# A fused attention and MoE kernel: the first round of scores starts with six query groups in place of eight, twelve tiles are drained in two halves of the keys, and narrow PSUM units last until unit 30

## The chip, the cores and the metric

The kernel runs on one core of a Trainium2 chip. A time is the device time of one execution of the whole program, in microseconds. The median over the runs shown is what counts; the profile is one further execution, recorded by the hardware profiler. The engines are TensorE (PE, with its weight loads as PEld), VectorE (DVE), ScalarE (ACT), GpSimd (POOL) and SyncE (SP). POOL and SP issue DMAs.

## The reference

An attention over pooled keys is followed by a two-layer network with a quick GELU, on every token.

```python
kv_pool = kv.reshape(B, H // r, r, W // r, r, C).mean(axis=(2, 4))   # r = 4
k = v = kv_pool.reshape(B, -1, C) @ w_sr
a = np.exp(s - s.max(-1, keepdims=True))       # s = (q @ k.T) / sqrt(C)
x = (a / (a.sum(-1, keepdims=True) + 1e-09)) @ v
h = x.reshape(B * S, D) @ w_in
out = (h * (1.0 / (1.0 + np.exp(-1.702 * h)))) @ w_out
```

B is 4, there are 12288 queries to an item, 768 pooled keys, C = 128 channels, and 2048 hidden units in the network. Inputs and output are float32; the kernel computes in bfloat16 with float32 sums.

## The kernel before

**Work and chunks.** The 49152 queries are cut into 96 groups of 512. For attention, a group and one block of 128 keys make a *chunk*: a matmul (`fill_attn`, L333) writes 128 x 512 scores to one PSUM bank. There are six key blocks, so six chunks to a group. For the network (called MoE in the code), a group and 128 of the 2048 hidden units make a chunk (`fill_moe`, L559), sixteen to a group. PSUM has eight banks of 512 float32 to a partition.

**Units.** ACT works on one to three chunks at once, a *unit*: an exponential for scores (L335), a GELU for MoE (L561). Units alternate between the banks 0 to 2 and 3 to 5, so that PE fills one while ACT empties the other. The banks 6 and 7 are accumulators for all other work of PE. A unit's result goes as bfloat16 to a frame of three slots in `ag`, an SBUF buffer of 102 slots. From there PE *drains* it: `drain_attn` (L344) multiplies the exponentials by the values, `drain_moe` (L569) by the second weight matrix. What lies in `ag` undrained is the lead that ACT has over PE.

**Draining.** An attention tile is 128 queries. Three tiles share an accumulator bank of 3 x 129 columns (the last column gives the sum for the softmax). A call `drain_attn(t, a)` does three of the six key blocks for tile t; both halves add up in the same bank. Then DVE takes the reciprocal (L355) and writes the product to `x` (L358). An MoE group of 512 queries sums 16 matmuls in one bank; DVE transposes it to `o_sb` (L580, three buffers) and SP stores it. The last group is drained by small matmuls (`drain_last`, L597), so that its parts can be stored one by one.

**Two rounds.** Groups 0 to 47 go through attention and MoE, then groups 48 to 95. Within the first round, eight groups start side by side: first their key blocks 0 and 1, then block 2 of all eight, block 3, and so on, because the keys arrive one block after another. After that the groups follow one by one. The first 18 units hold 1, 1, eight times 2, 3, 3, and twice 3, 3, 2 chunks, and all after that three (the last nine of the program two).

**Keys and queries at the start.** The first kv item is loaded in six chunks on POOL's DMA queue (`load_chunk`), between loads of the first four tiles of q (`load_q`, in halves or quarters of a tile; a half is two groups). For each kv chunk PE pools (`pool_chunk`, L134), DVE copies, PE makes keys and values (`key_and_value`, L156 and L157), and DVE copies them to SBUF (L158, L159). The queries of groups 0 to 15 are transposed on PE (`transpose_q`, L228) and copied by DVE (L234); later ones are cast to a DRAM buffer by POOL (`cast_q`) and loaded transposed by SP (`load_qT`), at the groups that `CAST` and `TURN` name. `gate` makes POOL wait for a small memset on DVE, so that such loads do not start too early.

**What sets the order.** All instructions are issued in an order that the program computes when it is built. The dictionary `first` names work that is put ahead of a given unit. For the rest a loop over units estimates, with fixed costs (`COST`, `FIXED`, `CHUNK`), when PE and ACT are free. After each `fill` it places drains and extras (pooling, transposing) as long as the next fill would not come late by its estimate (`limit`), or whenever few frames are left. Each engine then executes its own list in order.

**Work that ACT does not do.** Some chunks (`early`, `rolling`, `lent`) are computed on DVE by polynomials (L400 to L442), spread over the span.

## Time and profile before

| | |
|---|---|
| median of 4 runs | 954.76 us (954.69 to 954.86) |
| the profiled execution | 954.86 us |
| its span | 953.1 us |
| ACT busy | 934.6 us |
| PE busy | 941.8 us (ends of matmuls are modelled) |
| DVE busy | 513.1 us |
| first unit on ACT | starts at 9.44 us |
| switches between exponential and GELU | at 143.5, 488.9 and 605.9 us |

The page lists engines, a picture of the span in 40 slices, the chain of work that ended last, and groups of instructions by source line. The timeline gives instructions of one engine in order of time: start, length, engine, line, operation, output and input, how many were merged, and in brackets how long the engine was idle before and what ended that. Times in the trace are counted from the span's start. An ACT instruction is shown from its start to its last write, so the next starts before the one before it has ended; the pitch is the distance from start to start. A wait with several causes is put down to the one that came last.

### The profile page before, as it was taken

How to read it: one execution, taken by the hardware profiler on the slowest of the kernel's cores; microseconds unless marked ns; L12 is line 12 of the kernel's file. 1: busy time of each engine (PE TensorE's matmuls, PEld its weight loads, DVE VectorE, ACT ScalarE, POOL GpSimd, SP SyncE). 2: the span in 40 equal slices, each digit the busy share in tenths (PEclk: the TensorE clock that was granted, in tenths of full speed). 3: DMA queues.
4: the chain of work that ended last, by engine and by line, in shares of the span. 5: the costliest groups of instructions: out<-in, count | busy, mean ns of one | idle time of the engine just before them, and what ended most of it. 6: DMA issues, size and time to landing. Idle time of an engine off the chain costs nothing.

```text
span 953.1 us, 15440 instructions
## 1 busy us (share of the span) xinstructions
PE 941.8 (99%) x6330; PEld 504.1 (53%) x6330; DVE 513.1 (54%) x1004; ACT 934.6 (98%) x703; POOL 68.0 (7%) x118
## 2 busy tenths in 40 slices
PE   7899999999999999999999999999999999999998
PEld 4677777444444444454446777754444444444444
DVE  5443653111677877777545764367656555663011
ACT  5999999999999999999999999999999999999996
POOL 4101101330000332000000000000000000000000
PEclk9999999999999999999999999999999999999999
DMA  9989991999762799215268875563222222222222
GB/s 181 200 163 163 212 215 37 146 142 179 152 122 42 109 148 112 42 24 89 34 98 155 162 162 100 117 125 48 34 44 35 44 34 45 34 45 38 41 41 48
DMA packets 371319, 94.41 MB, mean 99 GB/s; under 512 B 344688, under 2 KB 368880, under 8 KB 370928
## 3 DMA queue, kind: packets, MB, share of 16 engines
q1 hardware_dynamic: 341808, 60.78, 36.8%
q0 software_dynamic: 29168, 32.51, 22.2%
q8 instruction: 49, 0.80, 0.4%
q14 instruction: 22, 0.18, 0.1%
q10 hardware_dynamic: 272, 0.13, 0.0%
HBM read 52.49 MB, written 48.23 MB: 106 GB/s over the span
## 4 chain that ended last, share of the span: by engine, by line
ACT 85%; PE 13%; DMA 1%; issue 0%; DVE 0%; POOL 0%; POOLq 0%
ACT ag L561 71%; ACT ag L335 14%; PE banks L344 6%; PE banks L333 5%; DMA x<-in_kv_dram 1%; PE banks L569 0%; PE banks L559 0%; PE banks L597 0%; PE banks L134 0%; DVE x L358 0%; PE banks L228 0%; ACT L561 0%; ACT L335 0%; POOL x L217 0%; PE banks L280 0%
## 5 line engine op out<-in xcount | busy, mean ns | idle before, releaser
L561 ACT ACTIVATE ag<-banks 128x1536 bf16<-128x1536 f32 (+1 forms) x511 | 683.2, 1507 | 0.0
L559 PE MATMUL banks<-x,w_in_sb 128*128 128x512 bf16 x1524 | 412.3, 379 | 0.1
L569 PE MATMUL banks<-ag,w_out_sb 128*128 128x512 bf16 x1508 | 407.2, 379 | 0.0
L335 ACT ACTIVATE ag<-banks 128x1536 bf16<-128x1536 f32 (+2 forms) x186 | 245.4, 1470 | 3.7 <-PE banks L333 3.6
L569 PEld LDWEIGHTS <-w_out_sb 128*128 128x128 bf16 x1520 | 148.6, 98 | 178.5 <-issue 0.2
L559 PEld LDWEIGHTS <-w_in_sb 128*128 128x128 bf16 x1524 | 147.0, 98 | 168.5 <-issue 2.1
L580 DVE STREAM_TRANSPOSE o_sb<-banks 128x512 f32<-128x512 f32 x95 | 67.9, 715 | 213.1 <-PE banks L569 199.3
L344 PEld LDWEIGHTS <-ag 128*128 128x128 bf16 x2272 | 145.4, 98 | 43.8 <-issue 1.1
L344 PE MATMUL banks<-v,ag 128*128 128x129 bf16 x2272 | 162.7, 220 | 0.2
L333 PE MATMUL banks<-qT,kT 128*128 128x512 bf16 x544 | 147.7, 379 | 4.0 <-ACT ag L335 2.3
L411 DVE SCALAR_TENSOR_TENSOR ea<-ea,eb 128x512 f32<-128x512 f32 x128 | 87.9, 687 | 3.9 <-DVE ea L411 0.8
L355 DVE RECIPROCAL rec<-banks 128x3 f32<-128x3 f32 x128 | 23.0, 180 | 98.4 <-PE banks L344 97.9
L358 DVE TENSOR_TENSOR x<-banks,rec 128x384 bf16<-128x384 f32 x128 | 71.4, 557 | 4.4
L333 PEld LDWEIGHTS <-kT 128*128 128x128 bf16 x544 | 46.7, 98 | 30.5 <-issue 3.9
L168 POOL DMA_DIRECT2D kvs<-in_kv_dram x32 | 40.3, 1299 | 31.0 <-DMA kvs<-in_kv_dram 28.7
L442 DVE RECIPROCAL eb<-ea 128x256 f32<-128x256 f32 x24 | 40.8, 1725 | 0.4
L400 DVE TENSOR_SCALAR ea<-banks 128x512 f32<-128x512 f32 x32 | 22.1, 692 | 33.8 <-PE banks L384 33.8
L490 POOL MEMSET gate_tile<- 1x1 f32 x39 | 4.2, 108 | 427.4 <-DVE gate_tile L489 427.4
L435 DVE SCALAR_TENSOR_TENSOR ea<-ea,eb 128x512 f32<-128x512 f32 x48 | 33.0, 688 | 1.4
L422 DVE TENSOR_SCALAR qT<-banks 128x512 f32<-128x512 f32 x12 | 8.3, 692 | 31.3 <-PE banks L378 31.1
L406 DVE SCALAR_TENSOR_TENSOR eb<-eb,ea 128x512 f32<-128x512 f32 x32 | 22.0, 687 | 0.8
L413 DVE SCALAR_TENSOR_TENSOR ag<-ea,ee 128x512 bf16<-128x512 f32 x24 | 16.6, 690 | 1.1
(80 smaller groups left out, 255.4 us busy)
## 6 DMA issues: line engine op xcount, KB each, us to landing
out_dram<-o_sb SPq DMA_DIRECT2D x380, 64.0 KB, 2.0
kvs<-in_kv_dram POOLq DMA_DIRECT2D x32, 384.0 KB, 6.3
q_bf<-in_q_dram POOLq DMA_DIRECT2D x20, 512.0 KB, 6.6
x_bf<-x SPq DMA_DIRECT2D x11, 768.0 KB, 6.1
x<-in_kv_dram POOLq DMA_DIRECT2D x12, 512.0 KB, 10.9
x_bf<-x SPq DMA_DIRECT2D x10, 384.0 KB, 4.7
x<-in_q_dram POOLq DMA_DIRECT2D x7, 256.0 KB, 15.1
w_in_sb<-in_moe_w_in_dram POOLq DMA_DIRECT2D x1, 512.0 KB, 7.8
```

Source lines behind the costliest of these rows:

```text
L168: nc.gpsimd.dma_start(out=kv_sums[b][:, i2], in_=kv_p[b, i, w, :, i2], **({"accum_op": ADD} if n else {}))
L333: nc.tensor.matmul(ps[:, k, :], kTs[i // GB][:, jc * 128:(jc + 1) * 128], rhs, start=True, stop=True)
L335: nc.scalar.activation(place([("a",) + c for c in chunks]), ps, AF.Exp, scale=scale)
L344: nc.tensor.matmul(av_of[u][:, k * (C + 1):(k + 1) * (C + 1)], weights(("a", i, jc))[:, o:o + T], vs[i // GB][:, jc, 0:C + 1], start=(jc = ...
L358: nc.vector.tensor_tensor(to, ps[:, :, 0:C], rec.unsqueeze(2).broadcast_to([128, TS, C]), MUL)
L411: nc.vector.scalar_tensor_tensor(a, a, COEFFS[k], b, ADD, MUL)
L435: nc.vector.scalar_tensor_tensor(a, a, COEFFS[k], b, ADD, MUL)
L442: nc.vector.reciprocal(b[:, m:m + 256], a[:, m:m + 256])
L559: nc.tensor.matmul(ps[:, k, :], w_in_sb[:, fc * 128:(fc + 1) * 128], x[:, g % (4 * XS) * G:(g % (4 * XS) + 1) * G], start=True, stop=True)
L561: nc.scalar.activation(place([("m",) + c for c in chunks]), ps, AF.Gelu_apprx_sigmoid)
L569: nc.tensor.matmul(o_of[g], w_out_sb[:, fc, :], weights(("m", g, fc)), start=(fc == 0), stop=(fc == FCH - 1))
L580: nc.vector.transpose(o_sb, o_of.pop(g))
```

## The change

- The accumulator may be any of several banks in turn (`turns`): 7, 6 and 5 from the start, and 2 as well from unit 4. Three units before the first unit of three chunks, banks 2 and 5 are taken out again. Bank 2 and 5 are free until then, because all units up to that one hold at most two chunks.
- The sizes of the units are 1, 1, then 28 times 2; from unit 30 on three chunks.
- Six groups start side by side in place of eight.
- The first 12 tiles (`SPLIT` = 4 sets of three) are drained in two halves of the keys: blocks 0 to 2 of all 12 tiles first, copied from PSUM to float32 partial sums (`parts`), then blocks 3 to 5, to which DVE adds the partial sums. The partial sums use the first frames of `ag`, which are kept out of use (`kept`) until the last set is done.
- The second half of q's second tile is loaded after kv chunks 2 to 4 in place of before them. The dictionary `first` names other units, and transpositions of groups 6 to 15 become extras.
- The builder's estimates are changed: how long a bank stays occupied includes DVE's queue (`copied`).
- Four casts and two transposing loads of q move from the last groups of the first attention round to MoE groups 19 to 22, 34 and 38.

```diff
--- before.py
+++ after.py
@@ -78,19 +78,22 @@
     banks = ppool.tile([128, 8, 512], F32, name="banks")
     closes = {}
-    free = {6: 0.0, 7: 0.0}
+    free = {2: 0.0, 5: 0.0, 6: 0.0, 7: 0.0}
+    turns = [7, 6, 5]
     last_acc = 7
     def acc(key=None):
         nonlocal last_acc
         last_acc = next_acc()
+        turns.append(last_acc)
+        turns.remove(last_acc)
         if key:
             closes[last_acc] = key
         return banks[:, last_acc, :]
     def next_acc():
-        return min((m for m in (13 - last_acc, last_acc) if m not in closes), key=lambda m: free[m])
+        return min((m for m in turns if m not in closes), key=lambda m: (max(free[m], now), turns.index(m)))
     def acc_bf():
         return acc().bitcast(BF)
@@ -100,6 +103,8 @@
             del closes[m]
             free[m] = then
+    now = 0.0
     x = xpool.tile([128, XS * SG], BF, name="x")
@@ -241,14 +246,13 @@
     load_chunk(0, 1)
     load_q(0, 2, 4)
     load_q(1, 0, 2)
-    load_q(1, 2, 4)
     for jc in range(2, JC):
         if jc == JC - 1:
-            load_q(2, 0, 2)
+            load_q(1, 2, 4)
         load_chunk(0, jc)
-    load_q(2, 2, 4)
-    load_q(3, 0, 2)
-    load_q(3, 2, 4)
+    for s in range(2, QS):
+        load_q(s, 0, 2)
+        load_q(s, 2, 4)
     cast_q(4)
     ones = cpool.tile([128, 32], BF)
@@ -289,12 +293,15 @@
     slot_of = {}
     low = 0
+    SPLIT = 4
+    kept = (2 * SPLIT + K - 1) // K
+    parts = ag[:, 0:2 * SPLIT, :].rearrange("p (u a) t -> p u (a t)", a=2).bitcast(F32)
     written = [0] * (AG // K)
     order, unit = [], 0
     def free_frames():
         busy = {s // K for s in slot_of.values()}
-        return [f for f in range(low // K, AG // K) if f not in busy]
+        return [f for f in range(max(low // K, kept), AG // K) if f not in busy]
     def place(chunks):
         nonlocal order, unit
@@ -336,21 +343,35 @@
     def drain_attn(t, a):
+        nonlocal kept
         i, u, k = t // 4, t // TS, t % TS
-        if k == a == 0:
+        split = u < SPLIT
+        if k == 0 and (a == 0 or split):
             av_of[u] = acc(("av", u))
         o = t % 4 * T
         for jc in range(a * K, a * K + K):
             nc.tensor.matmul(av_of[u][:, k * (C + 1):(k + 1) * (C + 1)], weights(("a", i, jc))[:, o:o + T],
-                             vs[i // GB][:, jc, 0:C + 1], start=(jc == 0), stop=(jc == JC - 1))
+                             vs[i // GB][:, jc, 0:C + 1], start=(jc == (a * K if split else 0)), stop=(jc == (a * K + K if split else JC) - 1))
             if t % 4 == 3 and (i, jc) in rolling:
                 used.append((i, jc))
             elif t % 4 == 3 and i not in early:
                 del slot_of["a", i, jc]
+        if k == TS - 1 and a == 0 and split:
+            close(("av", u), max(now, dve - 1.0) + 3.2)
+            on_dve(3.0)
+            nc.vector.tensor_copy(parts[:, u, 0:TS * (C + 1)], av_of.pop(u)[:, 0:TS * (C + 1)])
         if k == TS - 1 and a == 1:
             close(("av", u), max(now, dve - 1.0) + EVACUATE)
-            on_dve(4.3)
-            ps = av_of.pop(u)[:, 0:TS * (C + 1)].rearrange("p (k c) -> p k c", k=TS)
+            on_dve(6.5 if split else 4.3)
+            ps = av_of.pop(u)[:, 0:TS * (C + 1)]
+            if split:
+                part = parts[:, u, 0:TS * (C + 1)]
+                nc.vector.tensor_tensor(part, ps, part, ADD)
+                ps = part
+                if u == SPLIT - 1:
+                    kept = 0
+                    order.clear()
+            ps = ps.rearrange("p (k c) -> p k c", k=TS)
             rec = npool.tile([128, TS], F32, name="rec")
             nc.vector.reciprocal(rec, ps[:, :, C])
             n, o = divmod(u * TS, RT)
@@ -489,8 +510,8 @@
         nc.vector.memset(one, 0.0)
         nc.gpsimd.memset(one, 0.0)
-    TURN = {4: 4, 8: 5, 18: 6, 21: 7, 24: 8, 27: 9, 29: 10, 32: 11, 36: 12, 40: 13, 44: 14}
-    CAST = {0: 5, 4: 6, 13: 7, 19: 8, 22: 9, 25: 10, 28: 11, 32: 12, 36: 13, 40: 14, 44: 15, 46: 16}
+    TURN = {4: 4, 8: 5, 18: 6, 21: 7, 24: 8, 27: 9, 29: 10, 32: 11, 36: 12}
+    CAST = {0: 5, 4: 6, 13: 7, 19: 8, 22: 9, 25: 10, 28: 11, 32: 12}
     def background(i):
@@ -535,6 +556,11 @@
             order[:] = [f for f in order if f >= low // K]
         if g == 40:
             background(early[0])
+        if 19 <= g < 23:
+            gate()
+            cast_q(g - 6)
+        if g in (34, 38):
+            load_qT(13 + (g - 34) // 4)
         for b, lo in ((2, 2), (3, 24)):
             if lo <= g < lo + 8:
                 gate()
@@ -610,11 +636,11 @@
     NA, NM = NG * JC, NG * FCH
-    chunks, sizes = [], [1] * 2 + [2] * 8 + [3, 3] + [3, 3, 2] * 2
+    chunks, sizes = [], [1] * 2 + [2] * 28
     chunks += [(0, 0), (1, 0), (0, 1), (1, 1)]
-    chunks += [(i, jc) for i in range(2, 8) for jc in range(2)]
-    chunks += [(i, jc) for jc in range(2, JC) for i in range(8)]
-    chunks += [(i, jc) for i in range(8, NG) for jc in range(JC) if i not in early and (i, jc) not in rolling]
+    chunks += [(i, jc) for i in range(2, 6) for jc in range(2)]
+    chunks += [(i, jc) for jc in range(2, JC) for i in range(6)]
+    chunks += [(i, jc) for i in range(6, NG) for jc in range(JC) if i not in early and (i, jc) not in rolling]
     seq, todo = [], []
     todo_early = [("a", t, a) for t in range(NT) for a in range(2) if (t // TS * TS + TS - 1) // 4 in early]
     for n in range(R):
@@ -623,7 +649,11 @@
             m = sizes.pop(0) if sizes else K
             seq.append(("a", part[:m]))
             part = part[m:]
-        todo += [("a", t, a) for t in range(n * NT // R, (n + 1) * NT // R) for a in range(2)
+        begin = n * NT // R
+        if n == 0:
+            begin = SPLIT * TS
+            todo += [("a", t, a) for a in range(2) for t in range(begin)]
+        todo += [("a", t, a) for t in range(begin, (n + 1) * NT // R) for a in range(2)
                  if (t // TS * TS + TS - 1) // 4 not in early]
         flat = [(g, fc) for g in range(n * NG // R, (n + 1) * NG // R) for fc in range(FCH)]
         todo += [("m",) + c for c in flat]
@@ -634,6 +664,7 @@
             seq.append(("m", flat[:m]))
             flat = flat[m:]
+    narrow = min(p for p, (kind, part) in enumerate(seq) if len(part) == K)
     at = {}
     for p, (kind, part) in enumerate(seq):
         for c in part:
@@ -664,7 +695,7 @@
             f(*args)
             if f in COST:
                 now += COST[f][0]
-                free[last_acc] = now + COST[f][1]
+                free[last_acc] = copied(f)
         kind, part = seq[p]
         for i, jc in part:
             if (kind, i) not in begun:
@@ -674,7 +705,7 @@
                 f, *args = extras.pop(0)
                 now = max(now, free[next_acc()]) + COST[f][0]
                 f(*args)
-                free[last_acc] = now + COST[f][1]
+                free[last_acc] = copied(f)
     first = {
         0: [(pool_chunk, 0, 0), (transpose_q, 0), (warm, 1), (key_chunk, 0, 0), (transpose_q, 1)],
@@ -683,20 +714,17 @@
         3: [(transpose_q, 3)],
         4: [(transpose_q, 4)],
         5: [(transpose_q, 5)],
-        6: [(transpose_q, 6)],
-        7: [(transpose_q, 7)],
-        8: [(pool_chunk, 0, 2)],
-        9: [(key_and_value, 0, 2)],
-        11: [(pool_chunk, 0, 3)],
-        12: [(key_and_value, 0, 3)],
-        13: [(pool_chunk, 0, 4)],
-        14: [(key_and_value, 0, 4)],
-        15: [(transpose_q, 8)],
-        16: [(pool_chunk, 0, 5)],
-        17: [(key_and_value, 0, 5)],
-        18: [(transpose_q, 9)],
-        19: [(transpose_q, 10)],
-        20: [(transpose_q, 11), (later, 12), (later, 13), (later, 14), (later, 15)]}
+        6: [(pool_chunk, 0, 2)],
+        7: [(key_and_value, 0, 2)],
+        9: [(pool_chunk, 0, 3)],
+        10: [(key_and_value, 0, 3)],
+        12: [(pool_chunk, 0, 4)],
+        13: [(key_and_value, 0, 4)],
+        14: [(later, 6)],
+        15: [(pool_chunk, 0, 5)],
+        16: [(key_and_value, 0, 5), (later, 7)],
+        17: [(later, 8)],
+        18: [(later, g) for g in range(9, 16)]}
@@ -705,10 +733,11 @@
     COST = {pool_chunk: (1.9, 2.6), key_chunk: (0.3, 2.4), value_chunk: (0.3, 2.4),
             transpose_q: (1.05, 4.2), early_fill: (1.0, 5.5), key_and_value: (0.55, 3.5),
             transpose_pooled: (0.9, 3.6), make_k: (0.8, 3.2), make_v: (0.8, 3.7)}
+    COPY = {pool_chunk: 1.5, key_chunk: 1.5, value_chunk: 1.5, key_and_value: 2.8, transpose_q: 3.2}
     SMALL = 0.26
     RECIPROCAL = 10.5
     PAUSE = 4.0
-    now, end, extra_at = 0.0, [], 0.0
+    end, extra_at = [], 0.0
     source, dve = None, 0.0
     early_left = 2 * (G // T) * EARLY
@@ -716,6 +745,12 @@
         nonlocal dve
         dve = max(dve, now + 1.0) + cost
+    def copied(f):
+        if f not in COPY:
+            return now + COST[f][1]
+        on_dve(COPY[f])
+        return max(now + COST[f][1], dve)
     def fill(p):
         nonlocal now
@@ -723,6 +758,14 @@
             return
         kind, part = seq[p]
         prepare(p)
+        if p == 4:
+            turns.insert(0, 2)
+        if p == narrow - 3:
+            for m in (2, 5):
+                turns.remove(m)
+        if p == narrow:
+            assert not any(m in closes for m in (2, 5))
+            now = max(now, free.pop(2), free.pop(5))
         lo = K * (p % 2)
         (fill_attn if kind == "a" else fill_moe)(part, banks[:, lo:lo + len(part), :])
         if p >= 2:
@@ -753,7 +796,7 @@
             if f:
                 now = max(now, bank) + COST[f][0]
                 f(*args)
-                free[last_acc] = dve + 1.0 if f is early_fill else now + COST[f][1]
+                free[last_acc] = dve + 1.0 if f is early_fill else copied(f)
                 if f in (transpose_pooled, make_k, make_v):
                     on_dve(2.5)
                 extra_at = max(now + PAUSE, dve + 1.5 if f in (transpose_pooled, make_k, make_v) else 0.0)
@@ -773,8 +816,9 @@
             kind, i, c = source[0]
             needs = at[("at" if kind == "a" else kind, i, c)]
             cost = K * SMALL if kind == "a" else 1.0
-            first_of = c == 0 and (kind == "m" or i % TS == 0)
-            if source is not todo_early and (needs > n or (kind == "a" and first_of and at["at", i + TS - 1, 1] > n)
+            halved = kind == "a" and i // TS < SPLIT
+            first_of = (c == 0 or halved) and (kind == "m" or i % TS == 0)
+            if source is not todo_early and (needs > n or (kind == "a" and first_of and at["at", i + TS - 1, c if halved else 1] > n)
                                              or (kind == "m" and first_of and (i, FCH - 1) in lent
                                                  and made.get((i, FCH - 1), 1e9) > now + 1.0)
                                              or (kind == "a" and (early_waits(i) or first_of and early_waits(i + TS - 1)))):
@@ -795,7 +839,7 @@
                 early_left -= 1
                 if not early_left:
                     low = 0
-            if c == (1 if kind == "a" else FCH - 1) and (kind == "m" or i % TS == TS - 1):
+            if (halved or c == (1 if kind == "a" else FCH - 1)) and (kind == "m" or i % TS == TS - 1):
                 source = None
     assert not todo and not todo_early and not extras and not early_todo

```

## The prediction

> **What bounds the kernel now.** I read the engine totals first, then who ScalarE waits for, then the pitch of ScalarE's instructions, then the two ends of the span.
>
> ```profile
> span 953.1 us, 15440 instructions
> PE 941.8 (99%) x6330; PEld 504.1 (53%) x6330; DVE 513.1 (54%) x1004; ACT 934.6 (98%) x703; POOL 68.0 (7%) x118
> ...
> ACT 85%; PE 13%; DMA 1%; issue 0%; DVE 0%; POOL 0%; POOLq 0%
> ```
>
> ```profile
> ACT ag L335 <- PE banks L333: 3.6, 4, 2.2
> ```
>
> ACT is the bound: in the whole span it waits 3.6 us for scores (L333) in four places. So only three things can move the time: the number and width of ACT's instructions, new or removed waits of ACT, and what follows its last instruction. Pitch, from the ACT timeline and the chain:
>
> ```profile
> 16.08 1.03 ACT L335 ACTIVATE ag<-banks 128x1024 bf16<-128x1024 f32 x1
> ...
> 17.89 1.05 ACT L335 ACTIVATE ag<-banks 128x1024 bf16<-128x1024 f32 x1
> ...
> 284.60 14.63 ACT ag L561 x11
> ```
>
> Two narrow instructions (two chunks of 512) lie between 16.08 and 17.89: 0.904 us each. Eleven wide ones (three chunks) take 14.63: 1.331 each. A chunk thus costs 0.427, an instruction 0.050 besides.
>
> The early part on PE, and the landings of the loads:
>
> ```profile
> 17.59 0.56 PE L134 MATMUL banks<-sum,x 128*128 128x32 bf16 x16
> 18.08 0.59 PE L333 MATMUL banks<-qT,kT 128*128 128x512 bf16 x2
> 18.52 0.22 PE L156 MATMUL banks<-pTc,w_sr_sb 128*128 128x128 bf16 x1
> 18.58 0.22 PE L157 MATMUL banks<-w_sr_sb,pTc 128*128 128x128 bf16 x1
> 19.18 1.53 PE L333 MATMUL banks<-qT,kT 128*128 128x512 bf16 x5 [0.39 <-DVE kT L158]
> ```
>
> ```profile
> 12.36 0.71 POOL L217 DMA_DIRECT2D x<-in_q_dram  x1 [0.71 <-DMA x<-in_q_dram]
> 13.64 0.72 POOL L217 DMA_DIRECT2D x<-in_q_dram  x1 [0.57 <-DMA x<-in_q_dram]
> 14.92 0.70 POOL L217 DMA_DIRECT2D x<-in_q_dram  x1 [0.56 <-DMA x<-in_q_dram]
> 17.40 0.52 POOL L204 DMA_DIRECT2D q_bf<-in_q_dram  x1 [1.79 <-DMA x<-in_kv_dram]
> ```
>
> Each issue waits for the landing of the load eight places before it, and starts 0.28 after that (the trace's landing events: 12.07, 13.35, 14.63, 17.12). So a half tile of q takes 1.28 us in the queue, a chunk of kv 2.49.
>
> The end:
>
> ```profile
> 943.17 0.59 PE L559 MATMUL banks<-x,w_in_sb 128*128 128x512 bf16 x2
> 943.61 1.89 PE L569 MATMUL banks<-ag,w_out_sb 128*128 128x512 bf16 x8
> 945.33 0.67 PE L597 MATMUL banks<-w_out_sb,ag 128*128 128x128 bf16 x9
> 946.30 3.23 PE L597 MATMUL banks<-w_out_sb,ag 128*128 128x128 bf16 x55 [0.30 <-DVE o_sb L580]
> ```
>
> PE issues ACT's last unit at 943.17, and still has 8 output matmuls of 0.213 and all 64 small ones of the last group (0.053 each) to do. ACT ends at 944.96, PE at 949.53: the tail is PE's backlog. That is how work that is off ACT's path still sets the end.
>
> **The change, part by part.** The sum is made against the profiled execution, 954.86 us (span 953.1 and 1.76 around it), which is 0.10 above the median, 954.76.
>
> Narrow units. Round 1 had 2 units of one chunk, 10 of two and 88 of three; it gets 2, 28 and 76. Eighteen narrow ones more and twelve wide ones fewer: 18 x 0.904 - 12 x 1.331 = +0.30 us of ACT, uncovered, since ACT is the bound.
>
> The Trainium skill's page "ScalarE: Activation LUTs", section "What ACT_TABLE_LOAD costs", speaks harder against the change: a fixed 186 to 280 ns an instruction with 93 ns of overlap back to back, so by an estimate from it six more instructions would cost 0.56 to 1.12. The pitch above shows 0.050 each, so I keep 0.30.
>
> Start up to unit 5. The same instructions and the same loads in the same order; only accumulator banks differ. Unit 2 at 13.29 hangs on kv chunk 1 (landed 10.81). No gain: 0.
>
> Keys and values, units 6 to 16. With six groups, chunks 2, 3, 4, 5 of the keys are needed at units 7, 10, 13, 16 instead of 9, 12, 15, 18: dense, at 17.9, 20.6, 23.3 and 26.0 instead of 19.8, 23.4, 27.1 and 30.8. Moving the half tile of q behind them brings each chunk 1.28 earlier: 15.85, 18.28, 21.2, 24.9. From the first pooling matmul to the exponential took 17.59 to 19.82 = 2.23 us, so data are in time to about a third of a microsecond, except the last. But PE is in order. A narrow fill can start when the unit two before it is done (0.05 after its 1.03 us) and needs 0.62 to reach ACT, out of 2 x 0.904: 0.11 us of slack (wide: 0.33). A key/value step costs more: copying kT (L158) holds the fill until 0.66 after the key matmul. Before, this made unit 9 start 0.13 late (18.79, then 19.82). After, drains (attention x values, L344: six matmuls in 0.33) stand ahead of two of these steps, three ahead of another, and pooling (0.42) with a transposition (0.22) and three drains ahead of unit 15. Going along with these durations: unit 7 is 0.25 late, 10: 0.42, 12 and 13: 0.14 and 0.34, 15 and 16: 0.18 and 0.44; sum 1.77. From below: four times 0.13 = 0.52, if the drains hide in the waits. From above: 1.77 + 1.28 = 3.05, if chunk 5 lands as late as now. I take 1.7, as the order of the built program puts the drains in front.
>
> What these replace. Before, ACT loses 0.13, 0.13 and 0.10 at its own three key/value steps (19.8, 27.1, 30.8), and 0.38 at 37.94, where 12 drains and transpositions lie between two fills. The order there is another; I take -0.74, between -0.36 (the last stays in some form) and -0.99 (with 0.25 around 51 and 53).
>
> Two halves of the keys for 12 tiles. Four copies of 128x387 and four additions of the same size on DVE; the nearest row, L358 on 128x384, takes 0.557: 4.5 us in a stretch in which DVE is busy 3.35 of 9.0 us (22 to 31). Hidden by ACT's pace. If that cover is gone, PE's next drain or transposition waits for its bank, as at 36.53 (0.18 us, for L358), and behind it the fills. ACT waits for DVE too, at units 31 and 39, where it reuses frames that the partial sums used; those additions are about 2 us older, so 0.
>
> Later casts and loads. Four casts (0.5 us of POOL each) and two transposing loads leave the last third of round 1 and stand at MoE groups 19 to 22, 34 and 38. On SP two loads get in front of output stores, on POOL four casts behind gates get in front of the adding loads of kv. The load at 430.20 stands in just such a place: it holds SP for 5.51 us, and ACT runs on without a gap (12 units from 424.22 to 440.61). Cost 0; if DVE's output tiles ran out, some 5 us less the 7.1 us of a group times three tiles, still 0.
>
> The tail. The halves let PE drain in its early idle time (busy 6.76 of 9.0 between 22 and 31). In the order of the programs, filled chunks not yet drained are 12 fewer from unit 40 on (46 for 62 at unit 50), and the lead stays: after the last fill none of the 8 output matmuls is left, and 61 small ones for 64. That is 8 x 0.213 + 3 x 0.053 = 1.87 off the path; of the wait of 0.30 for the bank of the last whole group (L580) I estimate 0.15 gone. Taken: -2.0, between -1.7 and -2.2. Stores are no cover for it: the last one is issued right after PE's end and DVE's copy.
>
> Ten of ACT's 61 waits on its own semaphore go (51 are left); nothing in the profile prices one, so 0, at best -0.4 (units after one start 0.04 late on average).
>
> Sum: 0.30 + 1.7 - 0.74 - 2.0 = -0.74, so 954.12 for the profiled execution, **954.0 us** for the median. What this measurement tells from no change is taken as 0.2%, 1.9 us: "same" is 952.9 to 956.7.
>
> **Rivals.** A: the drains hide. The narrow stage then loses only 0.52, as the row at 19.82 has it, 37.94 goes too, and the sum is 0.30 + 0.52 - 0.99 - 2.2 = -2.4, with part of the semaphore waits -2.6: 952.2, faster. For it: between 13 and 19 us narrow units with a transposition each run at 0.904. Against: those have 0.22 between fills, the new ones up to 0.80.
>
> B: PE's queue stands behind DVE, slower. Each of the 20 units 9 to 28 with a drain or transposition into a bank that DVE has to empty pays the 0.18 of 36.53: 3.6 on top of 1.7, so 0.30 + 5.3 - 0.74 - 2.0 = +2.9: 957.7. It decides from a loss of 4.3 us in units 6 to 30. For it: 0.11 us of slack. Against: four banks in turn until unit 27, and DVE idle for more than half of the time.
>
> C: the tail does not follow, because PE reaches the end as late as before: 0.30 + 1.7 - 0.74 = +1.3, 956.0, same. Against: the order is fixed in the program, and PE at the end keeps ACT's pace.
>
> **How the numbers follow.** My forecast, within 1.9 us of before: 0.53; A 0.26; B 0.14; C 0.07. Mine alone spans 952.9 to 955.6, by 0.52 to 1.77 and the tail's bounds. The range reaches below A (0.30 + 0.52 - 0.99 - 0.4 - 2.2 = -2.8, 952.0, and half a microsecond for what I took as zero) and above C and most of B's approach (0.30 + 3.05 - 0.36 - 1.7 = +1.3, 956.0, and half of B's 1.7 above that): 951.5 to 957.0. Faster by over 0.2%: A and a little of mine, 0.27. Slower: B and a little of C, 0.16. Same: 0.57.
>
> **What would show it.** After: 703 ACTIVATE rows for 697 and no wait of ACT before 13.29 changed; ACT's wait for L333 grown from 3.6 by 1 to 2 us, all between 17 and 28, next to waits of L333 for kT; none at 37.9; no new ACT gap after 60 us; the last fill on PE followed by small matmuls alone, and from its start to the span's end 7.9 instead of 9.9. The prediction is wrong if ACT waits in many units up to 40 us (B), hardly at all (A), or for DVE or a load in the MoE stage.

## The result, and the profile after

The changed kernel takes **953.22 us** (median, 952.97 to 954.13), the kernel before 954.69 beside it: a ratio of 0.9983 with a 95% interval of 0.9979 to 0.9988. That is 0.17% faster, still inside the 0.2% that was called "same" beforehand, but at its edge, and 0.8 us below the predicted 954.0. The profiled execution took 953.18 us, against 954.86 for the one before.

The page of the changed kernel (span; engine totals; the chain's shares by engine):

```profile
span 951.4 us, 15449 instructions
PE 942.8 (99%) x6330; PEld 503.6 (53%) x6330; DVE 517.7 (54%) x1012; ACT 935.3 (98%) x709; POOL 68.3 (7%) x118
...
PE 77%; ACT 21%; DMA 1%; DVE 0%; issue 0%; POOL 0%; POOLq 0%
```

ACT has the six instructions more (709 for 703) and 0.7 us more to do. The chain's shares turned round, from ACT 85% to PE 77%, though both engines do almost what they did before. They run in step over the whole span, so a step back along the chain may go to either; shares like these don't say which is the bound. What ACT waits for does (waited for, total us, times, longest):

```profile
ACT ag L342 <- PE banks L340: 4.0, 5, 2.6
...
PE banks L139 <- DMA x<-in_kv_dram: 1.6, 2, 0.8
PE banks L340 <- DVE kT L163: 1.5, 4, 0.4
```

L342 and L340 are the exponential and the score matmul (L335 and L333 before). For its units ACT still waits in the first 28 us alone. PE's waits for kT, the copied keys, were 0.8 us in two places:

```profile
PE banks L333 <- DVE kT L158: 0.8, 2, 0.4
```

Now they are 1.5 us in four places, one at each key/value step. Two of them on PE (start, length, engine, line, what is done, count, idle time before), and the next units on ACT:

```profile
19.30 0.50 PE L353 MATMUL banks<-v,ag 128*128 128x129 bf16 x6
19.64 0.22 PE L161 MATMUL banks<-pTc,w_sr_sb 128*128 128x128 bf16 x1
19.70 0.22 PE L162 MATMUL banks<-w_sr_sb,pTc 128*128 128x128 bf16 x1
20.30 0.60 PE L340 MATMUL banks<-qT,kT 128*128 128x512 bf16 x2 [0.39 <-DVE kT L163]
...
22.69 0.33 PE L353 MATMUL banks<-v,ag 128*128 128x129 bf16 x3
22.87 0.22 PE L161 MATMUL banks<-pTc,w_sr_sb 128*128 128x128 bf16 x1
22.92 0.22 PE L162 MATMUL banks<-w_sr_sb,pTc 128*128 128x128 bf16 x1
23.53 0.60 PE L340 MATMUL banks<-qT,kT 128*128 128x512 bf16 x2 [0.39 <-DVE kT L163]
```

```profile
20.94 2.97 ACT L342 ACTIVATE ag<-banks 128x1024 bf16<-128x1024 f32 x3 [0.29 <-PE banks L340]
24.17 3.02 ACT L342 ACTIVATE ag<-banks 128x1024 bf16<-128x1024 f32 x3 [0.26 <-PE banks L340]
27.41 3.77 ACT L342 ACTIVATE ag<-banks 128x1024 bf16<-128x1024 f32 x4 [0.22 <-PE banks L340]
```

The drains (L353) stand ahead of the key matmuls, then comes the wait for kT, then the fill, and ACT has a gap. The gap in brackets is smaller than the loss, because an instruction is shown to its last write; the pitch gives 0.42 at the first of these. And the end of PE:

```profile
943.74 0.38 PE L595 MATMUL banks<-ag,w_out_sb 128*128 128x512 bf16 x1
943.95 0.33 PE L623 MATMUL banks<-w_out_sb,ag 128*128 128x128 bf16 x3
944.23 0.59 PE L585 MATMUL banks<-x,w_in_sb 128*128 128x512 bf16 x2
944.66 3.57 PE L623 MATMUL banks<-w_out_sb,ag 128*128 128x128 bf16 x61
```

After the last fill (L585, 944.23) only small matmuls are left, 61 of them, in one piece without the wait for `o_sb`.

Where the 1.7 us of the span came from (us; "lateness" is what ACT's pitches have above 0.477, 0.904 or 1.331 by width, added up over all units):

| | before | after | difference |
|---|---|---|---|
| unit 2 starts | 13.29 | 12.99 | -0.30 |
| ACT's units themselves (18 narrow more, 12 wide fewer) | | | +0.30 |
| lateness of all later units | 14.50 | 15.54 | +1.04 |
| last fill starts | 943.17 | 944.23 | +1.06 |
| last fill to PE's end | 6.36 | 3.99 | -2.37 |
| PE's end to the span's end | 3.54 | 3.19 | -0.35 |
| span | 953.07 | 951.41 | -1.66 |

### The profile page after: what moved, and what is told of

Read it like the earlier page. It is cut to its first block, busy times and chain, and to the rows that moved or that the text cites. A ratio compares the mean times of both kernels' runs of the same rounds, so it can differ in the third digit from the quotient of the medians.

```text
span 951.4 us, 15449 instructions
## 1 busy us (share of the span) xinstructions
PE 942.8 (99%) x6330; PEld 503.6 (53%) x6330; DVE 517.7 (54%) x1012; ACT 935.3 (98%) x709; POOL 68.3 (7%) x118
## 4 chain that ended last, share of the span: by engine, by line
PE 77%; ACT 21%; DMA 1%; DVE 0%; issue 0%; POOL 0%; POOLq 0%
PE banks L595 25%; PE banks L585 25%; ACT ag L587 20%; PE banks L353 13%; PE banks L340 12%; ACT ag L342 2%; DMA x<-in_kv_dram 1%; PE banks L139 0%; PE banks L623 0%; PE banks L405 0%; PE banks L399 0%; DVE kT L163 0%; POOL x L222 0%; PE banks L161 0%; PE banks L233 0%
## 5 line engine op out<-in xcount | busy, mean ns | idle before, releaser
L585 PE MATMUL banks<-x,w_in_sb 128*128 128x512 bf16 x1524 | 412.3, 379 | 0.1
L342 ACT ACTIVATE ag<-banks 128x1536 bf16<-128x1536 f32 (+2 forms) x192 | 246.3, 1440 | 4.4 <-PE banks L340 4.0
L585 PEld LDWEIGHTS <-w_in_sb 128*128 128x128 bf16 x1524 | 147.4, 98 | 171.2 <-issue 2.2
L353 PEld LDWEIGHTS <-ag 128*128 128x128 bf16 x2272 | 145.9, 98 | 45.8 <-issue 0.8
L353 PE MATMUL banks<-v,ag 128*128 128x129 bf16 x2272 | 163.9, 220 | 0.0
L340 PE MATMUL banks<-qT,kT 128*128 128x512 bf16 x544 | 148.7, 379 | 2.5 <-DVE kT L163 1.5
L379 DVE TENSOR_TENSOR x<-banks,rec 128x384 bf16<-128x384 f32 x124 | 69.1, 557 | 4.3
L340 PEld LDWEIGHTS <-kT 128*128 128x128 bf16 x544 | 46.3, 98 | 28.0 <-DVE kT L163 2.2
```

The costliest lines, as they stand in the source:

```text
L340: nc.tensor.matmul(ps[:, k, :], kTs[i // GB][:, jc * 128:(jc + 1) * 128], rhs, start=True, stop=True)
L342: nc.scalar.activation(place([("a",) + c for c in chunks]), ps, AF.Exp, scale=scale)
L353: nc.tensor.matmul(av_of[u][:, k * (C + 1):(k + 1) * (C + 1)], weights(("a", i, jc))[:, o:o + T], vs[i // GB][:, jc, 0:C + 1], start=(jc = ...
L379: nc.vector.tensor_tensor(to, ps[:, :, 0:C], rec.unsqueeze(2).broadcast_to([128, TS, C]), MUL)
L585: nc.tensor.matmul(ps[:, k, :], w_in_sb[:, fc * 128:(fc + 1) * 128], x[:, g % (4 * XS) * G:(g % (4 * XS) + 1) * G], start=True, stop=True)
```

## The experiments

Each is the changed kernel with one edit, unless it says otherwise. Times are medians. The runs were made on three chips; the kernel before, run beside them, took 954.64 to 954.67 us there. Ratios are to it. The terms of the sum come from each run's own profile.

**No halves.**

```diff
-    SPLIT = 4
+    SPLIT = 0
-    parts = ag[:, 0:2 * SPLIT, :]...
+    parts = None
```

> The changed kernel with no tiles in two halves (SPLIT = 0); six groups, narrow units, four banks, loads and casts as changed. In its program 8 output matmuls and all 64 small ones are left after the last fill, as before the change. My theory (the halves pay through PE's backlog at the end, and cost through drains ahead of the key/value steps): from the last fill to the span's end some 9.5 to 9.9 us in place of 7.2, that is +2.3 to +2.7; units 10, 12, 13 and 15 late by about 0.13, 0, 0.13 and 0.1 in place of 0.42, 0.12, 0.38 and 0.17, that is -0.7; together +1.6 to +2.0, about 955.0. Rival (the gain comes from the start: six groups, earlier kv chunks, more banks): the time stays within 0.3 of the changed kernel, or falls by the 0.7.

Measured: 954.90, ratio 1.0002 (0.9993 to 1.0011): all of the gain is gone. Its end on PE:

```profile
943.55 0.59 PE L585 MATMUL banks<-x,w_in_sb 128*128 128x512 bf16 x2
943.98 1.89 PE L595 MATMUL banks<-ag,w_out_sb 128*128 128x512 bf16 x8
945.71 0.67 PE L623 MATMUL banks<-w_out_sb,ag 128*128 128x128 bf16 x9
946.68 3.23 PE L623 MATMUL banks<-w_out_sb,ag 128*128 128x128 bf16 x55 [0.31 <-DVE o_sb L606]
```

The 8 large matmuls and the wait are back as before, and the tail is 2.34 longer. PE is busy for 7.12 of the 9.0 us between 22 and 31, for 8.23 with the halves. Against that, lateness is 0.86 smaller. Of this 0.42 lies up to unit 45: without drains ahead of the keys, units 10, 12 and 13 together lose 0.16 in place of 0.92. Unit 15 did not go as expected. It is 0.49 late, not 0.1, because PE now waits 0.36 us there for chunk 5, which landed at 24.84. The other 0.45 lies in units 46 to 100, and no run tells what makes it. So the halves give 2.34 at the end and take 0.86 before it.

**Narrow units until 18.**

```diff
-    chunks, sizes = [], [1] * 2 + [2] * 28
+    chunks, sizes = [], [1] * 2 + [2] * 16
```

> The changed kernel with narrow units up to unit 18 in place of 30 (8 wide for 12 narrow). In its program 6 output matmuls and 64 small ones are left after the last fill. My theory: -0.2 for four ACT instructions fewer, units 6 to 16 as in the changed kernel, +1.9 at the tail; +1.5 to +1.9, 955.0. Rival (narrow units are only a cost after the keys are there): -0.2, 953.0.

Measured: 955.00, ratio 1.0004 (0.9995 to 1.0013).

```profile
944.13 0.59 PE L585 MATMUL banks<-x,w_in_sb 128*128 128x512 bf16 x2
944.57 1.46 PE L595 MATMUL banks<-ag,w_out_sb 128*128 128x512 bf16 x6
945.86 0.67 PE L623 MATMUL banks<-w_out_sb,ag 128*128 128x128 bf16 x9
946.83 3.23 PE L623 MATMUL banks<-w_out_sb,ag 128*128 128x128 bf16 x55 [0.31 <-DVE o_sb L606]
```

Twelve narrow units fewer save ACT 12 x 0.904 - 8 x 1.331 = 0.20, which 0.23 more lateness takes away again, and the tail is 1.89 longer. The extra banks go at unit 15, three before the first wide unit; PE is busy 0.86 us less between 22 and 50 (25.94 for 26.80) and brings six matmuls to the end. Together with the next run this says that narrow units are worth their price for the banks that they leave free.

**Two accumulator banks.**

```diff
-    free = {2: 0.0, 5: 0.0, 6: 0.0, 7: 0.0}
-    turns = [7, 6, 5]
+    free = {6: 0.0, 7: 0.0}
+    turns = [7, 6]
```

and the lines at units 4 and 27 and at the first wide unit, which add and remove banks 2 and 5, left out.

> The changed kernel with two accumulator banks (7 and 6) throughout, as before the change. In its program 8 output matmuls and 64 small ones are left after the last fill. My theory: the tail as before the change, 9.3 to 9.7 us for 7.0 to 7.3, and the units 6 to 16 late by about as much as in the changed kernel (1.6); +2.0 to +2.6, 955.5. Rival (banks matter little, since DVE empties them in time): within 0.4 of the changed kernel.

Measured: 956.91, ratio 1.0024 (1.0015 to 1.0033), 3.7 us above the changed kernel: the direction expected, and 1.4 us more. PE's waits for DVE:

```profile
21.56 0.50 PE L353 MATMUL banks<-v,ag 128*128 128x129 bf16 x6 [0.22 <-DVE ag L362]
...
26.30 0.55 PE L139 MATMUL banks<-sum,x 128*128 128x32 bf16 x16 [0.78 <-DVE qT L239]
```

```profile
24.56 1.94 ACT L342 ACTIVATE ag<-banks 128x1024 bf16<-128x1024 f32 x2 [0.61 <-PE banks L340]
27.33 1.02 ACT L342 ACTIVATE ag<-banks 128x1024 bf16<-128x1024 f32 x1 [0.83 <-PE banks L340]
```

This is rival B, PE's queue behind DVE's emptying of a bank, as it would have been without the extra banks. It makes the units up to 45 late by 3.61 us in sum, for 2.26 (unit 15 alone 0.95 for 0.17). The other 2.31 are the tail, 8 large matmuls and the wait again. Its stretch from 22 to 31, then that of the changed kernel (stretch, length, busy us of PE, PEld, DVE, ACT and POOL, granted clock, DMA share, GB/s):

```profile
22.00:31.00 9.00, 6.87 (x87) 4.36 (x84) 4.29 (x11) 7.16 (x8) 0.52 (x2) 1.00 1.21 223
```

```profile
22.00:31.00 9.00, 8.23 (x103) 5.44 (x100) 5.79 (x14) 8.46 (x9) 0.52 (x2) 1.00 1.18 216
```

The same stretch of the kernel before:

```profile
22.00:31.00 9.00, 6.76 (x68) 3.91 (x69) 3.35 (x10) 9.00 (x9) 0.49 (x1) 1.00 1.21 226
```

PE is busy 8.23 us with four banks and 6.87 with two; before the change it was 6.76. Halves and narrow units without the banks leave PE as idle as it was.

**Eight spare matmuls on PE.** Their results are not used.

```diff
+        if 14 <= g < 22:
+            extras.append((spare,))
+    def spare():
+        nc.tensor.matmul(acc(), w_in_sb[:, 0:128], x[:, 0:G], start=True, stop=True)
```

> The changed kernel with eight spare matmuls of 128x512 added on PE, one in each of the MoE groups 14 to 21 (240 to 300 us), where PE is 300 units away from both ends; their results are not read. ACT's instructions are the same. In the program's order 11 output matmuls and 64 small ones are then left after the last fill. My theory (any work of PE, wherever it stands, comes out at the tail, as PE has no time of its own left): 8 x 0.213 = 1.7 by the work alone, 2.5 to 2.9 by the order at the end, so 955.0 to 956.0, ACT's starts unchanged. Rival (PE has slack in the MoE stage, where it is drawn as busy 99% only because ends are modelled): within 0.3 of the changed kernel.

Measured: 956.66, ratio 1.0021 (1.0012 to 1.0030), 3.4 above the changed kernel and 0.7 above the top of what was expected.

```profile
944.63 0.59 PE L589 MATMUL banks<-x,w_in_sb 128*128 128x512 bf16 x2
945.06 2.54 PE L599 MATMUL banks<-ag,w_out_sb 128*128 128x512 bf16 x11
947.43 0.67 PE L627 MATMUL banks<-w_out_sb,ag 128*128 128x128 bf16 x9
948.40 3.23 PE L627 MATMUL banks<-w_out_sb,ag 128*128 128x128 bf16 x55 [0.31 <-DVE o_sb L610]
```

Work put on PE between 245 and 295 us comes out after the last fill: the tail is 3.07 longer. That is 11 x 0.215 for the large matmuls, 3 x 0.053 for the small ones, 0.06 at the very end, and 0.49 for the whole-group bank: 0.31 of shown wait and about 0.18 in which PE starts again. Only 1.72 of this is the eight matmuls themselves; the order that the builder then makes leaves three more behind. The tail is all but 0.4 of the difference. The rest is ACT reaching its last unit later, which was not expected: single units are late, such as the one that starts at 545.4 us, by 0.35.

**The old order of the loads.**

```diff
+    load_q(1, 2, 4)
     for jc in range(2, JC):
         if jc == JC - 1:
-            load_q(1, 2, 4)
+            load_q(2, 0, 2)
         load_chunk(0, jc)
```

> The changed kernel with the old order of loads: the second half of q's second tile ahead of kv chunks 2 to 4. My theory: each kv chunk lands 1.28 us later, chunk 2 then arrives about 1.3 too late for unit 7, and the later ones only as late as that: ACT loses about +1.3 at unit 7 and nothing more, 954.5. Rival (data are early enough, PE's order sets unit 7): +0.2 at most.

Measured: 955.40, ratio 1.0010 (1.0002 to 1.0019), 2.2 above the changed kernel and 0.9 above what was expected. The profiled execution is one of its longer ones, 956.58. On PE, and then the granted clock (the third number from the end) us by us:

```profile
16.71 0.57 PE L139 MATMUL banks<-sum,x 128*128 128x32 bf16 x16 [1.24 <-DMA x<-in_kv_dram]
...
20.66 0.60 PE L139 MATMUL banks<-sum,x 128*128 128x32 bf16 x16 [1.24 <-DMA x<-in_kv_dram]
...
22.56 0.31 PE L161 MATMUL banks<-pTc,w_sr_sb 128*128 128x128 bf16 x1
```

```profile
20.00:21.00 1.00, 0.34 (x13) 0.35 (x14) 0.00 (x0) 0.90 (x1) 0.11 (x1) 0.85 1.02 204
21.00:22.00 1.00, 0.78 (x12) 0.45 (x10) 0.29 (x1) 0.00 (x0) 0.48 (x2) 0.50 1.16 194
22.00:23.00 1.00, 0.98 (x8) 0.71 (x7) 0.00 (x0) 0.85 (x1) 0.23 (x1) 0.50 1.22 228
23.00:24.00 1.00, 0.64 (x2) 0.28 (x3) 0.49 (x2) 0.17 (x1) 0.26 (x1) 0.50 1.11 222
```

The order of the loads is needed, as expected: in this execution units 6 and 9 are 1.22 and 1.37 late. Two things made it dearer than expected. The wait for chunk 2 did not cover that for chunk 3, which landed at 20.61. And PE's clock then fell to half: a 128 x 128 matmul took 0.31 in place of 0.22, and unit 10 was 1.31 late for 0.42.

The late landing does not come from the changed kernel. From the same place in the queue chunk 3 landed at 19.56 in the profile of the kernel before, but at 20.66 and 20.43 in two further profiles with that kernel's first loads (its variants below). The clock fell in some executions only. Of the eleven, the four whose mean granted clock was 0.996 to 0.998 are the longest, 955.73 to 957.31 us; the other seven, at 0.999 or 1.000, took 954.69 to 955.48. So the clock does not explain the median's 0.9 above what was expected; the landing of chunk 3 may, but the one profile of this kernel is of an execution in which the clock fell.

**Key/value steps ahead of the drains.** The steps that `first` names are issued right after the previous fill.

```diff
+    def ahead(p):
+        nonlocal now
-        for f, *args in first.get(p, ()):
+        for f, *args in first.pop(p, ()):
...
         fill(n + 2)
+        lets = 0.0
+        if n >= 3:
+            if any(f is key_and_value for f, *_ in first.get(n + 3, ())):
+                lets = 1.6
+            ahead(n + 3)
...
-            limit = end[-1] - K - HANDOVER if n + 3 < len(seq) else 1e9
+            limit = end[-1] - K - HANDOVER + lets if n + 3 < len(seq) else 1e9
```

> The changed kernel, with the pooling and key/value steps of units 6 to 16 issued right after the fill before, ahead of the drains and transpositions, and the drains allowed into the time in which the kT copy holds the next fill. The program's end is the same (61 small matmuls after the last fill). My theory (the drains ahead of the steps made units 10, 12, 13, 15, 16 late): these are late by about 0.15, 0, 0.15, 0.05, 0.2 in place of 0.42, 0.12, 0.38, 0.17, 0.34; -0.9, 952.3. Rival (the steps are late from the DVE copies and bank waits alone, whatever stands ahead): 0, within 0.2.

Measured: 952.32, ratio 0.9975 (0.9966 to 0.9985), 0.9 below the changed kernel. The time came as expected, but not by the steps that were forecast, so the agreement is in part luck. PE's waits for kT went from 1.5 us to 0.4 and unit 10 from 0.42 to 0.08, but unit 15 from 0.17 to 0.74. In the profiled execution the first 45 units are as late in sum as in the changed kernel (2.27 for 2.26), and 0.70 was gained in units 46 to 100. Unit 15 hangs on the load:

```profile
25.52 0.57 PE L139 MATMUL banks<-sum,x 128*128 128x32 bf16 x16 [1.12 <-DMA x<-in_kv_dram]
```

Chunk 5 landed at 25.48 here and at 24.93 in the changed kernel's run. With the drains out of the way, the load is the next limit, as it was for unit 15 without halves.

**The same with chunk 5 a place earlier, and six sets in halves.**

```diff
     for jc in range(2, JC):
-        if jc == JC - 1:
-            load_q(1, 2, 4)
         load_chunk(0, jc)
+    load_q(1, 2, 4)
...
-    SPLIT = 4
+    SPLIT = 6
...
-        14: [(later, 6)],
-        16: [(key_and_value, 0, 5), (later, 7)],
-        17: [(later, 8)],
+        16: [(key_and_value, 0, 5)],
+        17: [(later, 6), (later, 7), (later, 8)],
```

> The run before (steps ahead of the drains) with two edits more: the second half of q's second tile is loaded after kv chunk 5, so that this lands 1.28 us earlier, with the transpositions of groups 6 to 8 planned from unit 17 on; and 18 tiles in halves in place of 12, which keeps the end at 61 small matmuls. In the run before, unit 15 became late by 0.74, with PE waiting 1.12 us for chunk 5. My theory now (with the drains out of the way, the landing of chunk 5 is what holds units 15 and 16): units 13, 15 and 16 together late by 0.5 in place of 1.3, PE's wait for kv loads down from 3.2 to about 2 us, time 951.5. Rival (the units are late from PE's own order): unchanged at 952.3.

Measured: **951.84**, ratio 0.9971 (0.9959 to 0.9982), the best version: 2.8 us below the kernel before and 1.4 below the changed one. Chunk 5 landed at 23.66, PE did not wait for it, and units 15 and 16 are late by 0.08 together, where the changed kernel has 0.51. PE's wait for kv loads is 2.8 us, not 2, but 2.6 of it is for chunks 0 and 1, before unit 2. The other two edits were not run by themselves: unit 16 may gain from the transpositions that now stand behind it, and what the two further sets in halves do to the time stays open. On PE:

```profile
24.49 0.56 PE L139 MATMUL banks<-sum,x 128*128 128x32 bf16 x16
25.16 0.59 PE L339 MATMUL banks<-qT,kT 128*128 128x512 bf16 x2
25.59 0.22 PE L161 MATMUL banks<-pTc,w_sr_sb 128*128 128x128 bf16 x1
```

The lateness per unit (us) in these runs:

| unit | after | no halves | two banks | keys first | and chunk 5 |
|---|---|---|---|---|---|
| 7 | 0.21 | 0.24 | 0.21 | 0.24 | 0.24 |
| 10 | 0.42 | 0.08 | 0.42 | 0.08 | 0.08 |
| 12 and 13 | 0.50 | 0.08 | 1.06 | 0.44 | 0.45 |
| 15 and 16 | 0.51 | 0.79 | 1.25 | 1.04 | 0.08 |

**Casts and loads back, and the end of the span.**

```diff
+    TURN = {..., 36: 12, 40: 13, 44: 14}
+    CAST = {..., 32: 12, 36: 13, 40: 14, 44: 15, 46: 16}
-        if 19 <= g < 23:
-            gate()
-            cast_q(g - 6)
-        if g in (34, 38):
-            load_qT(13 + (g - 34) // 4)
```

> The changed kernel with the four casts and two transposing loads back in the last third of round 1. My theory: 0, within 0.2, since ACT waits for none of them. Rival (the relief of the DMA queues between 100 and 143 us, or of SP at the switch to MoE, gives part of the gain): +0.4 or more, seen as gaps of ACT between 110 and 160 us.

Measured: 953.58, ratio 0.9989 (0.9980 to 0.9997), 0.36 above the changed kernel. The units' lateness is that of the changed kernel to a hundredth, so neither theory's place was right: ACT did not notice. The difference lies behind PE's last matmul, 3.55 us to the span's end for 3.19, and in the kernel before it is 3.54. The trace shows a pause there of 0.34 to 0.36 between two drain instructions of SP. Four runs asked what sets it: four column loads more on SP, four pairs of small memsets more on DVE and POOL (both with the casts back), and in the kernel before the casts and loads moved alone, or the four loads alone. The edits:

```diff
+    def pad(k):
+        nc.sync.dma_start(out=pads[:, k:k + 1], in_=w_sr[:, k:k + 1])
+        if 12 <= g < 16:
+            pad(g - 12)
```

```diff
+        if 19 <= g < 23:
+            gate()
```

> The four casts and two loads back in round 1, and four loads of one column (512 bytes) more on SP, at MoE groups 12 to 15. Theory S, the number of instructions on SP sets the end: in the traces so far SP's first and second drain after the last store lie 0.06 apart where SP has 598 to 600 instructions (the changed kernel and seven of its variants), and 0.34 to 0.36 apart where it has 595 (the kernel before, and the variant with casts and loads back). With 599 the distance is 0.06 again, from PE's last matmul to the span's end 3.15 to 3.25, and the time 953.2. Rival, the place of the casts and loads sets it: 0.35, 3.55 and 953.6, as with casts and loads back alone.

> The four casts and two loads back in round 1, and four pairs of small memsets on DVE and POOL more, at MoE groups 19 to 22, so that POOL has the 147 instructions of the changed kernel and SP the 595 of before. Theory S: the distance of SP's drains stays 0.35, the end 3.55, the time 953.6. Rival, POOL's number of instructions sets it: 0.06, 3.2 and 953.2.

> The kernel before with the move of the casts and loads alone (no halves, eight groups, eighteen narrow units less). SP gets two instructions more, 597. The prediction put this move at 0: 954.65 and a distance of 0.34 between SP's drains, if 597 is still short of the limit of theory S. If the limit lies below 597, or if the place of casts and loads sets the end: 0.06, from PE's last matmul to the end 3.2 for 3.54, and 954.3.

> The kernel before with four loads of one column more on SP at MoE groups 12 to 15, 599 instructions on SP, casts and loads where they were. Theory S: the distance of SP's drains falls from 0.34 to 0.06 and the time by as much, to 954.35. Rival, the place of casts and loads, or chance from run to run: 0.34 and 954.65.

Measured, in us (pause: the largest gap around SP's 592nd recorded instruction; counts are of the profile's records):

| | SP's records | time | ratio, interval | SP's pause is before | PE's end to span's end |
|---|---|---|---|---|---|
| before | 595 | 954.67 | | second drain | 3.54 |
| after | 598 | 953.22 | 0.9983 (0.9979 to 0.9988) | a wait, store still under way | 3.19 |
| casts back | 595 | 953.58 | 0.9989 (0.9980 to 0.9997) | second drain | 3.55 |
| casts back, 4 on SP | 599 | 953.79 | 0.9991 (0.9982 to 0.9999) | a wait, store landed | 3.71 |
| casts back, 4 on POOL | 595 | 953.52 | 0.9988 (0.9980 to 0.9997) | second drain | 3.55 |
| before, casts moved | 598 | 954.36 | 0.9997 (0.9989 to 1.0006) | a wait, store still under way | 3.23 |
| before, 4 on SP | 596 | 954.88 | 1.0001 (0.9992 to 1.0010) | first drain | 3.82 |

POOL's number of instructions is ruled out. Theory S was right about the drains, which lie 0.06 apart with 599 and 596, and wrong about the end, which grew. Four loads more gave the kernel before only one record more, 596 where 599 were expected. The pause did not vanish with them: it came at another instruction, and the waits after the store stood in another order, more of them after its landing (the first drain at 2.87 and at 2.87, for 2.30). SP's last store stands earlier or later by as many records as the count says, and in every row the pause, 0.34 to 0.36, is right before SP's 592nd record. The rows fit this reading: if SP is waiting for its last store anyway (it lands 2.2 us after PE's end), the pause is covered; if not, it is added to the span. Moving the casts and loads gives SP three waits more and puts the pause into that cover: the kernel before gains 0.31 us by this alone (954.36 for 954.67), and its own profile has 3.23 for 3.54. The medians are finer than the ratios' intervals here; that the difference is real rests on the pause in the traces. What the pause is, no run shows. The Trainium skill, page "Runtime: NRT & Kernel Launch", section "Instruction fetch mechanics", says that an engine's instructions are refilled in blocks of 256 and that crossing into the next is mostly hidden; a fixed place in SP's stream would fit that, but the rows above don't show a fetch, and 592 is no multiple of 256 in the records that the profile has. Whatever it is, here it is not hidden when it falls behind the last store.

## Why the prediction was right or wrong

**Which case.** The forecast case came about. In A the drains would have hidden and the key/value units lost 0.52; they lost 1.64. B's waits for DVE appear only with two banks. C did not come about either: PE follows ACT to its last unit and has less left, and the shorter end outweighs the 1.36 us by which ACT's narrow and late units put off the last fill.

**Narrow units, +0.30.** Six more instructions, and nothing in the runs contradicts 0.050 us each: in the changed kernel narrow units in a row (17 to 21) also start 0.904 apart. ACT's busy time grew by 0.7, overlap included.

**Keys and values, +1.7.** Right in size and place. By unit, 7, 10, 12, 13, 15 and 16 were predicted at 0.25, 0.42, 0.14, 0.34, 0.18 and 0.44, in sum 1.77, and were 0.21, 0.42, 0.12, 0.38, 0.17 and 0.34, in sum 1.64. For units 10, 12 and 13 the drains are shown as the cause: without them these lose 0.08, 0 and 0.08. Unit 7 is late by 0.21 to 0.24 in the table whatever is edited, so the drains are not its cause. At 15 and 16 more than the drains is at work: without them unit 15 waits for chunk 5, and only in the run with that chunk earlier does the lateness of both go. The landings were predicted at 15.85, 18.28, 21.2 and 24.9 and came at 15.51, 17.98, 21.16 and 24.93.

**What these replace, -0.74.** Units 9, 15 and 18 and the 0.38 at 37.9 are gone. Lateness in all grew by 1.04, where 1.7 - 0.74 made 0.96; up to unit 45 it grew by 0.93, with a new 0.20 at unit 30 in it.

**Start, 0.** Unit 2 began 0.30 earlier, which is no effect of the change: with the same first loads and units it began between 12.78 and 13.29 in the 14 profiles.

**Halves on DVE, 0.** Held with four banks. With two, the cover is gone and PE waits 0.22 and 0.78.

**The tail, -2.0.** The mechanism was right, the term too small. From the last fill to PE's end -2.37 was measured, 2.34 longer without the halves. The large and the small matmuls are 8 x 0.215 + 3 x 0.053 = 1.88, as predicted. The step that failed was the half of the wait of 0.30 for L580's bank: the last whole group is now closed before the last fill, so the whole wait went, and with it the 0.18 in which PE started again, 0.49 in place of 0.15.

**Casts and loads, 0.** The step that failed: "on SP two loads get in front of output stores" was priced on ACT alone. ACT indeed saw nothing, but SP's stream changed by three waits, and its pause at the end went under cover: -0.31 by the run on the kernel before, -0.35 in the sum. The prediction looked at when the last store is issued, not at what SP does after it.

**The sum.** Against the predicted -0.74 for the span, -1.66 was measured: -0.30 at the start, -0.37 and -0.35 at the end, and +0.10 between (lateness 1.04 for 0.96, and rounding). In the medians, 953.22 for 954.0, the two terms of the end make up the difference. The span that the prediction gives its own case, 952.9 to 955.6, does not come out of the bounds it names: 0.30 + 0.52 - 0.74 - 2.2 makes 952.6 and 0.30 + 1.77 - 0.74 - 1.7 makes 954.4. The measured time lies inside either.

**What would show it.** The tail, the waits for kT and the quiet MoE stage came as named, and 7.9 from the last fill to the end was 7.2. The sign that failed is ACT's row for its waits: 3.6 was to grow by 1 to 2 us and grew to 4.0, which by the prediction's own words would have spoken for A. A gap counts there only from the last write of the instruction before, so a unit that is 0.13 late shows none; the pitch has to be read.

## What to carry to other kernels

Where two engines run in step, the work that one of them has left after the other's last instruction is a sum over the whole program: move work into its earliest idle time, and count the instructions after the last fill. Early drains paid here only with banks of their own, and they paid more once the work that a later fill needs was issued ahead of them. A difference of a few tenths that shows in no stage may lie after the last matmul: follow the issuing engine to its last record.

## What the runs showed of the hardware that was not expected

- **SP's pause.** Of the 14 profiles, 11 show SP standing still for 0.34 to 0.36 us right before its 592nd recorded instruction, wherever the last store stands relative to it; in the other three SP waits 0.63 to 0.70 at that place.
- **The clock after short waits.** With the loads in the old order PE waited twice for 1.24 us and was busy for 1.79 of the 3.41 us from 17.29 to 20.70. Then the trace's record of the granted clock has 0.50 for 3.41 us, from 20.70 to 24.12. The Trainium skill, page "TensorE: Matmul & The Clock Gate", section "What's actually happening", has the clock halved after an idle window of about 3.4 us; here it fell with no idle stretch of that length, the longest near it being 1.24. The share of busy time does not decide it alone: in the best version PE stood still for 1.83 us ahead of 7.06, was busy for 1.62 of the 3.41 us from 3.61 to 7.02, and kept 1.00. Where the limit lies stayed open.
- **The last part of a load.** From the landing of a chunk's first part to that of its last took 0.3 to 2.0 us in the 14 profiles. With the old order of loads the first part of chunk 3 landed at 18.72 to 18.75 in four profiles, the last at 19.56 in that of the kernel before and at 20.43 to 20.66 in the other three. What sets this lag stayed open.
